# Two smaller buffers for the sums of the expert stage, and one sum written over its input

## The chip, the cores and the metric

The kernel runs on one core of a Trainium2 chip. The metric is the time of one execution on the device, in microseconds (us), as a median over runs; less is better. Profiles are of one further execution each.

## What is computed

Three parts follow each other. The output of the first is split up by tokens for the second, and the output of the second is the input of the third (N = 12288 tokens, width 256):

```python
# attention, per batch of 3072 tokens
attn = np.maximum(matmul(z, z.T) / S, 0.0) ** 2
x = u * matmul(attn, v)
# experts: each token goes to the one expert of 8 with the largest logit
h = np.maximum(x[mask] @ w1[e], 0.0)
out[mask] = gate_w[mask, None] * eom[mask, e, None] * (h @ w2[e])
# gated MLP with a product over the sequence
h = np.maximum(x @ w_in, 0.0)
u, v = h[..., :512], h[..., 512:]
v_n = (v - mean(v)) / sqrt(var(v) + 1e-6)
v_s = einsum('ts,bsd->btd', w_spatial, v_n) + b_spatial[None, :, None]
return (u * v_s) @ w_out
```

## The kernel before

The kernel holds every product as three matmuls of high and low parts. The product with w_spatial is made by a scheme with seven products in place of eight, on two levels, and that scheme needs sums and differences of blocks of w_spatial. They depend on no other input, so they are made early, as side work: `first_sums` beside the attention, and `spatial_sums` (from L714 on) beside the experts. Their results go to tensors in HBM, `w_sums` and `w_parts`, which the last part reads.

The experts run in `moe` (L602). 8 experts have 4 chunks of up to 512 tokens each, and each chunk has 8 steps f, so there are 256 steps i. A step makes on PE the first layer of (c, f) into a PSUM bank (L667 to L669), on ACT `hh` (L671), on DVE `hlo` (L673), and then on PE the second layer of two steps earlier (L620 to L622, called l2 below), which reads that earlier step's hh and hlo. When f is 7 the second layer's accumulators are emptied, by ACT (L630) and by DVE (L632) in turn, and an indirect transfer of POOL's queue scatters each to `y_tok` (L494). At the end of a step side work is pumped: one piece each of four generators, and `spatial_sums` is the last of them. A piece ends at a `yield`.

`spatial_sums` runs over 2 halves tb and 6 blocks k. For each k two rounds (th) load four tiles of 128 x 768 on SP's queue (L727, in the order a21, a22, a11, a12; a11 and a21 are of the tiles `sa` with four buffers, a22 and a12 of `sb` with three), make four whole sums on DVE (L731, L734, L736, L738), two of which POOL's queue stores to `w_sums` (L732, L739). The a11 of both rounds are then S2, the a21 of both rounds S3. Two groups follow, i = 1 on S2 and i = 2 on S3. A group splits its two tiles into halves of 384 columns (a11, a12 of the first, a21, a22 of the second), stores three of them as they are and makes four more blocks on DVE, L751, L754, L757 and L760, one in each of four pieces; every put (L747) is a transfer of POOL's queue to `w_parts`. Three of the four sums go to a tile `so` that has one buffer; the fourth, L754, writes over a21.

The order on PE, ACT, DVE and SP is that in which the program is written. POOL's order is made by a scheduler. Each engine's queue is worked off in order, and an instruction that waits holds up all that stand behind it. A tile's buffer is given to its next user when its last readers are done, transfers included.

Of the kernel before, what the change touches and what calls it, by code (L numbers as in the profile page):

```python
# [27 lines left out]
F32 = mybir.dt.float32  # L28
# [4 lines left out]
ALU = mybir.AluOpType  # L33
AX = mybir.AxisListType

P = 128
# [18 lines left out]
class _Kernel:  # L55
# [658 lines left out]
    def spatial_sums(self):  # L714


        nc, wk, tt = self.nc, self.big, self.nc.vector.tensor_tensor
        flat = self.sw.rearrange("n (s k) p t -> n k p s t", s=2)
        for tb in range(2):
            for k in range(6):  # L720
                S2, S3 = [], []
                for th in range(2):
                    tbs = 2 * th + tb
                    a11, a21 = (wk.tile([P, 768], F32, name="sa", bufs=4) for _ in range(2))
                    a22, a12 = (wk.tile([P, 768], F32, name="sb", bufs=3) for _ in range(2))
                    for dst, r, c in ((a21, 1, 0), (a22, 1, 1), (a11, 0, 0), (a12, 0, 1)):
                        nc.sync.dma_start(dst.rearrange("p (s t) -> p s t", s=2), self.wsq[r, c, tbs, k])  # L727
                    yield
                    yield
                    cs = slice(tbs * 384, tbs * 384 + 384)  # L730
                    tt(a22, a21, a22, op=ALU.add)  # L731
                    nc.gpsimd.dma_start(flat[0, k][:, :, cs], a22.rearrange("p (s t) -> p s t", s=2))  # L732
                    yield
                    tt(a21, a11, a21, op=ALU.subtract)  # L734
                    yield
                    tt(a11, a22, a11, op=ALU.subtract)  # L736
                    yield
                    tt(a12, a12, a11, op=ALU.subtract)  # L738
                    nc.gpsimd.dma_start(flat[1, k][:, :, cs], a12.rearrange("p (s t) -> p s t", s=2))  # L739
                    yield  # L740
                    S2.append(a11)
                    S3.append(a21)
                for i, (q, r) in ((1, S2), (2, S3)):
                    o = wk.tile([P, 1152], F32, name="so", bufs=1)
                    s1, s2, s4 = (o[:, n * 384 : n * 384 + 384] for n in range(3))
                    (a11, a12), (a21, a22) = ((t[:, 0:384], t[:, 384:768]) for t in (q, r))
                    put = lambda m, t: nc.gpsimd.dma_start(self.parts(i, m, tb, k), t)  # L747
                    put(1, a11)
                    put(2, a12)
                    put(4, a22)  # L750
                    tt(s1, a21, a22, op=ALU.add)  # L751
                    put(5, s1)
                    yield
                    tt(a21, a11, a21, op=ALU.subtract)  # L754
                    put(7, a21)
                    yield
                    tt(s2, s1, a11, op=ALU.subtract)  # L757
                    put(6, s2)
                    yield
                    tt(s4, a12, s2, op=ALU.subtract)  # L760
                    put(3, s4)
                    yield

    def produce(self):
# [598 lines left out]
```

## Time and profile before

| | us |
|---|---|
| median of 2 timed runs | 3648.74 (3648.63 to 3648.86) |
| the profiled execution | 3639.52 |
| its span, from first to last instruction | 3637.4 |
| attention, in that span | 0 to about 1186 |
| experts | about 1186 to 1842 |
| gated MLP | about 1842 to 3637 |

Times in the views are microseconds from the start of the span, if not marked ns. PE is the matmul engine, PEld its loading of weights, DVE the vector engine, ACT the scalar engine, POOL GpSimd, SP the sync engine; SP and POOL issue the transfers here (SPq and POOL in the rows). L751 is line 751 of the kernel. "out<-in" gives the tiles by the program's names.

### The profile page before, as it was taken

How to read it: one execution, taken by the hardware profiler on the slowest of the kernel's cores; microseconds unless marked ns; L12 is line 12 of the kernel's file. 1: busy time of each engine (PE TensorE's matmuls, PEld its weight loads, DVE VectorE, ACT ScalarE, POOL GpSimd, SP SyncE). 2: the span in 40 equal slices, each digit the busy share in tenths (PEclk: the TensorE clock that was granted, in tenths of full speed). 3: DMA queues.
4: the chain of work that ended last, by engine and by line, in shares of the span. 5: the costliest groups of instructions: out<-in, count | busy, mean ns of one | idle time of the engine just before them, and what ended most of it. 6: DMA issues, size and time to landing. Idle time of an engine off the chain costs nothing.

```text
span 3637.4 us, 48879 instructions
## 1 busy us (share of the span) xinstructions
PE 3522.8 (97%) x17680; PEld 3018.9 (83%) x17680; DVE 2507.1 (69%) x4541; ACT 1689.9 (46%) x2948; POOL 633.9 (17%) x861
## 2 busy tenths in 40 slices
PE   7999999999998899999999989999999999999999
PEld 6787787887886888989978879999988888888887
DVE  7989888888887567755557867576665556545544
ACT  6766777777775233333234443333333333323322
POOL 3213212113111334444322210000000000000000
PEclk9999999999999899999999999999999999999999
DMA  8212211102000666666447776768674567655543
GB/s 287 70 64 72 74 52 48 40 30 70 30 24 19 219 219 229 218 223 211 159 159 283 279 270 233 246 204 283 208 266 164 187 221 247 233 170 174 200 151 116
DMA packets 227454, 604.75 MB, mean 166 GB/s; under 512 B 24560, under 2 KB 62720, under 8 KB 227200
## 3 DMA queue, kind: packets, MB, share of 16 engines
q1 hardware_dynamic: 160032, 373.71, 30.7%
q0 software_dynamic: 67168, 227.81, 16.8%
q8 instruction: 140, 2.29, 0.3%
q14 instruction: 114, 0.93, 0.1%
HBM read 393.08 MB, written 208.35 MB: 165 GB/s over the span
## 4 chain that ended last, share of the span: by engine, by line
PE 77%; issue 8%; DVE 5%; DMA 5%; POOL 3%; ACT 2%; SPq 0%; DVEq 0%; POOLq 0%; ACTq 0%
PE bank L1212 7%; PE bank L1213 7%; PE bank L1211 7%; PE bank L228 6%; PE bank L229 6%; PE bank L227 5%; PE bank L1116 4%; PE bank L1115 4%; PE bank L1117 4%; PE bank L263 3%; PE bank L264 3%; PE bank L667 2%; PE bank L620 2%; PE bank L668 2%; PE bank L669 2%
## 5 line engine op out<-in xcount | busy, mean ns | idle before, releaser
L228 PE MATMUL bank<-lo,G 128*128 128x512 f32 x1152 | 455.9, 396 | 21.6 <-DVE lo L272 21.4
L1158 DVE TENSOR_TENSOR wl<-raw,wh 128x512 fp32r<-128x512 f32 x288 | 198.8, 690 | 397.4 <-ACT wh L1157 394.9
L272 DVE TENSOR_TENSOR lo<-a,hi 128x512 fp32r<-128x512 f32 x576 | 416.1, 722 | 76.1 <-PE bank L264 1.5
L266 ACT ACTIVATE r<-bank 128x512 f32<-128x512 f32 x576 | 343.1, 596 | 268.2 <-PE bank L264 244.1
L270 DVE TENSOR_TENSOR a<-r 128x512 f32<-128x512 f32 x576 | 414.0, 719 | 57.6 <-ACT r L266 56.5
L229 PE MATMUL bank<-hi,G 128*128 128x512 f32 x1152 | 452.6, 393 | 0.0
L227 PE MATMUL bank<-hi,G 128*128 128x512 f32 x1152 | 451.7, 392 | 0.0
L1157 ACT ACTIVATE wh<-raw 128x512 fp32r<-128x512 f32 x288 | 181.6, 631 | 534.3 <-PE bank L1213 484.4
L268 ACT ACTIVATE hi<-r 128x512 fp32r<-128x512 f32 x576 | 364.7, 633 | 18.3
L671 ACT ACTIVATE hh<-bank 128x512 fp32r<-128x512 f32 (+2 forms) x256 | 132.7, 519 | 431.6 <-PE bank L669 424.0
L1212 PE MATMUL bank<-wl,R 128*128 128x512 f32 x792 | 311.8, 394 | 2.1 <-DVE wl L1158 2.1
L1213 PE MATMUL bank<-wh,R 128*128 128x512 f32 x792 | 311.9, 394 | 0.0
L1211 PE MATMUL bank<-wh,R 128*128 128x512 f32 x792 | 311.9, 394 | 0.0
L228 PEld LDWEIGHTS bank<-lo,G 128*128 128x128 f32 x1152 | 217.5, 189 | 82.1 <-DVE lo L272 35.6
L673 DVE SCALAR_TENSOR_TENSOR hlo<-bank,hh 128x512 fp32r<-128x512 f32 (+2 forms) x256 | 150.9, 589 | 195.3 <-ACT hh L671 194.5
L227 PEld LDWEIGHTS bank<-hi,G 128*128 128x128 f32 x1152 | 217.2, 189 | 48.6 <-ACT hi L268 0.2
L229 PEld LDWEIGHTS bank<-hi,G 128*128 128x128 f32 x1152 | 217.4, 189 | 45.6
L1115 PE MATMUL bank<-wh,R 128*128 128x384 f32 x640 | 216.2, 338 | 13.5 <-ACT R L933 13.5
L620 PE MATMUL bank<-G,hh 128*128 128x256 f32 x728 | 208.0, 286 | 15.7 <-DVE in L632 15.0
L1116 PE MATMUL bank<-wl,R 128*128 128x384 f32 x640 | 216.1, 338 | 1.7 <-DVE wl L1184 1.7
L1117 PE MATMUL bank<-wh,R 128*128 128x384 f32 x640 | 215.9, 337 | 0.0
L399 POOL DMA_INDIRECT x_slots<-rows,slot x96 | 112.2, 1169 | 589.7 <-ACT r L266 519.0
(285 smaller groups left out, 8558.3 us busy)
## 6 DMA issues: line engine op xcount, KB each, us to landing
v_ops<-vu POOLq DMA_DIRECT2D x84, 512.0 KB, 4.5
raw<-w_parts SPq DMA_DIRECT2D x108, 384.0 KB, 3.5
ra<-v_ops SPq DMA_DIRECT2D x75, 512.0 KB, 4.4
raw<-wsp SPq DMA_DIRECT2D x72, 512.0 KB, 3.7
raw<-w_sums SPq DMA_DIRECT2D x72, 512.0 KB, 4.0
xin<-partial SPq DMA_DIRECT2D x60, 512.0 KB, 5.5
u_hid<-vu POOLq DMA_DIRECT2D x48, 512.0 KB, 3.9
ur<-u_hid SPq DMA_DIRECT2D x48, 512.0 KB, 6.9
```

The costliest lines, as they stand in the source:

```text
L227: nc.tensor.matmul(acc[d], vh[:, c], hi, start=(k == 0), stop=False)
L228: nc.tensor.matmul(acc[d], vh[:, c], lo, start=False, stop=False)
L229: nc.tensor.matmul(acc[d], vl[:, c], hi, start=False, stop=(k == NK - 1))
L268: nc.scalar.activation(hi, r, AF.Square)
L270: nc.vector.tensor_tensor(a, r, r, op=ALU.mult)
L272: nc.vector.tensor_tensor(lo, a, _f(hi), op=ALU.subtract)
L1115: nc.tensor.matmul(ps, vh, wh[:, ws], start=(k == 0), stop=False)
L1116: nc.tensor.matmul(ps, vh, wl[:, ws], start=False, stop=False)
L1117: nc.tensor.matmul(ps, vl, wh[:, ws], start=False, stop=(k == 5))
L1211: nc.tensor.matmul(acc[d], vh, wh, start=(k == 0), stop=False)
L1212: nc.tensor.matmul(acc[d], vh, wl, start=False, stop=False)
L1213: nc.tensor.matmul(acc[d], vl, wh, start=False, stop=(k == 11))
```

## The change

`so` becomes a tile of two blocks in place of three, with two buffers in place of one. The third sum of a group, L760, is written over its input a12, and put(3) sends a12. The sizes of the other tiles, the loops and the pieces stay.

```diff
                 for i, (q, r) in ((1, S2), (2, S3)):
-                    o = wk.tile([P, 1152], F32, name="so", bufs=1)
-                    s1, s2, s4 = (o[:, n * 384 : n * 384 + 384] for n in range(3))
+                    o = wk.tile([P, 768], F32, name="so", bufs=2)
+                    s1, s2 = (o[:, n * 384 : n * 384 + 384] for n in range(2))
                     (a11, a12), (a21, a22) = ((t[:, 0:384], t[:, 384:768]) for t in (q, r))
                     put = lambda m, t: nc.gpsimd.dma_start(self.parts(i, m, tb, k), t)
                     put(1, a11)
...
                     put(6, s2)
                     yield
-                    tt(s4, a12, s2, op=ALU.subtract)
-                    put(3, s4)
+                    tt(a12, a12, s2, op=ALU.subtract)
+                    put(3, a12)
                     yield
```

No row of an engine moves on PE, ACT, DVE and SP; what rows wait for does. DVE, where the first k's group i = 1 ends and group i = 2 begins (DMASW is a transfer of POOL's queue, DMAHW one of SP's, the other names are engines):

```order
 L673 SCALAR_TENSOR_TENSOR hlo<-bank_67,hh 128x512 [waits Activation_49]
 L185 TENSOR_TENSOR G_115<-raw_12936,G_114 128x512 [waits Activation_49]
-L760 TENSOR_TENSOR so<-sa,so 128x384 [waits DVE_49]
+L760 TENSOR_TENSOR sa<-sa,so 128x384 [waits DMASW5_49,DVE_49]
 L673 SCALAR_TENSOR_TENSOR hlo<-bank_66,hh 128x384 [waits Activation_49]
-L751 TENSOR_TENSOR so<-sa 128x384 [waits DMASW3_49,DMASW5_49,DMASW1_49,DVE_49]
+L751 TENSOR_TENSOR so<-sa 128x384
 L673 SCALAR_TENSOR_TENSOR hlo<-bank_67,hh 128x384 [waits Activation_49]
 L632 TENSOR_SCALAR in_13075<-bank_68,gate 128x256 [waits PE_49]
```

The three transfers are off the row of L751, and one is on the row of L760.

SP, a little later, the four loads of the second k's second round and what stands around them:

```order
 L504 DMA rows<-x_slots 128x1032 [waits PE_49]
-L727 DMA sa<-wsq 128x768 [waits DMASW5_49,DMASW3_49,DVE_49]
+L727 DMA sa<-wsq 128x768 [waits DMASW3_49,DVE_49]
 L727 DMA sb<-wsq 128x768 [waits DMAHW7_49,DMASW0_49]
-L727 DMA sa<-wsq 128x768 [waits DMAHW0_49,DVE_49]
+L727 DMA sa<-wsq 128x768 [waits DMAHW0_49,DMASW5_49,DVE_49]
 L727 DMA sb<-wsq 128x768 [waits DMAHW1_49,DMAHW2_49,DMASW6_49,DVE_49]
 L504 DMA rows<-x_slots 128x1032 [waits PE_49]
```

The third load, that of a11, has a transfer of POOL's queue added to what it waits for. The names DMASW are eight counters that are used in turn.

POOL, around the end of the first k's group i = 1 (a scatter is L494, a load of expert weights L419):

```order
 L747 DMA w_parts<-so 128x384 [waits DMASW3_49,DVE_49]
 L419 DMA raw_13547<-w 128x1024 [waits DMASW4_49,DVE_49]
-L747 DMA w_parts<-so 128x384 [waits DMASW5_49,DVE_49]
-L494 DMA y_tok<-in_13075,ids 26624x256 [waits DMASW6_49,Activation_49]
-L747 DMA w_parts<-so 128x384 [waits DMASW7_49,DVE_49]
-L494 DMA y_tok<-in_13075,ids 26624x256 [waits DMASW0_49,Activation_49]
+L747 DMA w_parts<-sa 128x384 [waits DMASW5_49,DVE_49]
+L747 DMA w_parts<-so 128x384 [waits DMASW6_49,DVE_49]
+L494 DMA y_tok<-in_13075,ids 26624x256 [waits DMASW7_49,Activation_49]
+L494 DMA y_tok<-in_13075,ids 26624x256 [waits DMASW0_49,DVE_49]
```

The put of the new first sum (`so`) stands ahead of the scatters instead of among them; the put ahead of it is the one that sends a12, of `sa`.

## Rows read from the trace of the kernel before

**Rows 1.** The page: the span, and each engine's busy time.

```profile
span 3637.4 us, 48879 instructions
PE 3522.8 (97%) x17680; PEld 3018.9 (83%) x17680; DVE 2507.1 (69%) x4541; ACT 1689.9 (46%) x2948; POOL 633.9 (17%) x861
```

**Rows 2.** Windows: length, busy PE, PEld, DVE, ACT, POOL, PE's clock, DMA share, GB/s.

```profile
1200.00:1843.00 643.00, 613.01 (x4163) 577.74 (x4162) 398.08 (x753) 208.63 (x421) 257.84 (x348) 0.98 0.58 201
1560.00:1595.00 35.00, 35.00 (x258) 34.22 (x257) 23.09 (x43) 11.61 (x26) 14.74 (x21) 1.00 0.62 223
```

**Rows 3.** Waits from 1200 to 1843: who, for whom, total, times, longest.

```profile
DVE so L751 <- DMA w_parts<-so: 46.6, 10, 8.8
...
PE bank L620 <- DVE in L632: 21.5, 5, 6.6
...
PE bank L667 <- DVE hlo L673: 7.7, 3, 3.6
DVE so L751 <- issue: 6.7, 1, 6.7
```

**Rows 4.** Timeline of DVE: start, length, work, idle time ahead of it.

```profile
1234.74 0.55 DVE L760 TENSOR_TENSOR so<-sa,so 128x384 f32<-128x384 f32 x1
...
1245.30 0.56 DVE L751 TENSOR_TENSOR so<-sa 128x384 f32<-128x384 f32 x1 [8.83 <-DMA w_parts<-so]
...
1246.24 0.87 DVE L632 TENSOR_SCALAR in<-bank,gate 128x256 f32<-128x256 f32 x2
...
1252.14 0.55 DVE L760 TENSOR_TENSOR so<-sa,so 128x384 f32<-128x384 f32 x1
```

**Rows 5.** Timeline of POOL, whose instructions here issue transfers.

```profile
1200.63 1.11 POOL L747 DMA_DIRECT2D w_parts<-sa  x2
1203.42 1.07 POOL L747 DMA_DIRECT2D w_parts<-sa  x2 [1.68 <-DVE sa L736]
...
1237.91 0.54 POOL L747 DMA_DIRECT2D w_parts<-so  x1
...
1252.98 0.55 POOL L747 DMA_DIRECT2D w_parts<-so  x1 [1.18 <-DVE so L760]
```

**Rows 6.** Timeline of PE around the same stall.

```profile
1238.85 0.28 PE L621 MATMUL bank<-K,hh 128*128 128x256 f32 x1
1238.97 0.28 PE L622 MATMUL bank<-K,hlo 128*128 128x256 f32 x1
...
1246.86 0.55 PE L620 MATMUL bank<-K,hh 128*128 128x256 f32 x1 [6.57 <-DVE in L632]
1247.21 0.42 PE L621 MATMUL bank<-K,hh 128*128 128x256 f32 x1
1247.43 0.41 PE L622 MATMUL bank<-K,hlo 128*128 128x256 f32 x1
```

**Rows 7.** Windows of the seven stretches at a lower clock: the first, and the sum.

```profile
1242.80:1253.00 10.20, 6.14 (x26) 6.17 (x27) 4.25 (x9) 0.49 (x1) 4.75 (x7) 0.50 0.34 133
...
sum 30.60, PE 26.17 PEld 25.34 DVE 19.73 ACT 3.49 POOL 16.85; mean PE 3.74 PEld 3.62 DVE 2.82 ACT 0.50 POOL 2.41
```

**Rows 8.** Landing of `so` puts; L754's durations in ns (min/median/max).

```profile
DMA to landing us min/median/max: 2.1/3.7/8.7
...
L754 DVE TENSOR_TENSOR sa<-sa x24: 546/549/573, 1229.0 to 1807.9; 128x384 f32<-128x384 f32 x24
```

**Rows 9.** SP's loads at L727: their landing, and the timeline of one.

```profile
DMA to landing us min/median/max: 2.9/4.7/10.5
...
1235.33 0.33 SPq L727 DMA_DIRECT2D sa<-wsq  x1
```

**Rows 10.** Timeline of DVE: from an L760 to the next L734.

```profile
1502.06 0.55 DVE L760 TENSOR_TENSOR so<-sa,so 128x384 f32<-128x384 f32 x1
...
1506.13 0.56 DVE L751 TENSOR_TENSOR so<-sa 128x384 f32<-128x384 f32 x1 [1.82 <-DMA w_parts<-so]
...
1518.07 0.94 DVE L734 TENSOR_TENSOR sa<-sa 128x768 f32<-128x768 f32 x1
```

## The prediction

> **What bounds the kernel now.** I read the page's busy line first: PE is busy for 97% of the span, DVE for 69%, POOL for 17% [rows 1]. A change in DVE or POOL work moves the end only where PE stands still for it. So the next view is the stretch in which the changed lines run, the experts, from 1200 to 1843 us: 643.00 us long, PE busy in 613.01 of them [rows 2]. PE loses 30.0 us there. A stretch between the losses is busy in every microsecond (35.00 of 35.00), with POOL and DVE at work as elsewhere [rows 2]. So what makes PE stop is something that happens at some places only.
>
> The table of waits says what [rows 3]. PE's own waits in this stretch are 21.5 us at L620 for DVE's L632 (5 times) and 7.7 us at L667 for the hlo of L673 (3 times): 29.2 of the 30.0 us are waits for DVE. DVE's row in the same table is L751 `so<-sa`, the first sum of a group: 46.6 us in 10 waits for the landing of a `w_parts<-so` transfer, and 6.7 us in one more whose ender is not named: 53.3 us in 11 waits.
>
> One of them in order of time [rows 4]: L760 of the first group runs at 1234.74; L751 of the second group, one hlo later in DVE's queue, runs at 1245.30, after 8.83 us of idle time. The reason is the one buffer of `so`: the second group's s1 goes where the first group's s4 has just been written, so it may start only when put(3) has read s4 out. POOL issued that put at 1237.91 [rows 5], so it took some 7 us to land. Behind L751 on DVE stand an hlo and the two L632 that empty the accumulators of l2. PE goes on at 1246.86 after 6.57 us of idle time, 0.6 us after the first L632 [rows 6].
>
> The stall has a second price. The granted clock is 0.50 of full from 1242.80 to 1253.00, that is 1.2 GHz and not 2.4, after PE had stood still; six later stalls leave 3.4 us each. The seven stretches are 30.60 us and hold 26.17 us of PE work [rows 7]. Behind the stall it takes 0.22 us from the start of an L621 to that of the L622 after it, against 0.12 us ahead of it [rows 6].
>
> **The change, step by step.**
>
> *The wait of L751 goes.* With two buffers of `so` a group writes where the group before last has written, a whole k earlier. The order of DVE shows it: the row of L751 waited for three transfers and waits for none. All 24 groups lose the wait; 11 of them had stalled. What comes back on PE is the idle time, 30.0 us, and the slow clock. At half clock a stretch of PE work takes twice as long, so 26.17 us of it at 0.50 are 13.1 us lost. Sum: 30.0 + 13.1 = 43.1 us.
>
> Here a rule of the Trainium skill can be set beside the rows. The page "TensorE: Matmul & The Clock Gate", section Terms, puts the penalty of a throttled clock at the throttled time times the share of pulses left out. The stretches together are 30.60 us, which by that would be 15.3 us, and the sum 45.3. I go by the PE work inside them, since 4.4 of these microseconds are idle time that stands in the 30.0 already.
>
> *The rows of DVE, ACT and PE stay in their places.* No instruction is added. L760 now writes over one of its inputs; L754 does that already, and takes 549 ns in the middle [rows 8] against the 0.55 us of an L760 [rows 4]. Cost: nothing.
>
> *L760 waits for put(2).* It overwrites a12, which put(2) sends out, so it now waits for that transfer. Price if it were just behind: up to 8.7 us, the longest landing of a `so` put [rows 8], at 24 places. Where the put stands: POOL's order is made by the scheduler and not by hand, and it issues puts 1 and 2 as soon as the whole sums of L734 and L736 are there. In the trace these are two pairs of `w_parts<-sa` [rows 5]: the one at 1203.42, released by L736, is of the first group, 31 us ahead of its L760 at 1234.74; the one at 1200.63 is of the second, 51 us ahead of its L760 at 1252.14 [rows 4]. Cost: nothing; the cover is over three times the longest landing.
>
> *SP's third load waits for put(3).* The tile that holds a12 is loaded anew for the next k. Before, that load needed only DVE's L760 to be over (SP issued it at 1235.33 [rows 9], the moment L760 ended); now it needs the landing of put(3). The order of SP shows the added transfer on the third of four loads. Behind it in SP's queue stand one more load, the `rows` of a later chunk, and the next group's loads. The delay: POOL issues put(3) some 0.3 to 2.6 us after L760 (1234.74 + 0.55 to 1237.91 is 2.6, 1252.69 to 1252.98 is 0.3 [rows 4, 5]), and it lands 2.1 to 8.7 us later, 3.7 in the middle [rows 8]. So 2.4 to 11.3 us, then the load itself: 4.7 us in the middle, 10.5 at the longest [rows 9]. Who waits for it: DVE at L734. The shortest distance that I found between an L760 and the L734 that needs the load is 1502.61 to 1518.07, 15.5 us, and a stall of 1.82 us inside it goes, which leaves 13.6 [rows 10]. In the middle 0.3 + 3.7 + 4.7 = 8.7 us are needed, so 4.9 are left over; at the worst of everything, 21.8, the load is 8.2 us late there. The other distances are longer. I take 0 to 1 us in all, nearest to the middle values, and keep the bound from the other side for the range.
>
> *POOL.* The put of s4 becomes a put of a12, of the same 128 x 384 numbers. In its queue put(5) of the second group now stands ahead of a chunk's scatters and so ahead of them waits for L751; but L751 itself comes some 9 us earlier than the 1245.30 of [rows 4]. POOL is busy 17% of the span; nothing is added there.
>
> The sum, against the profiled execution: 3639.5 (span 3637.4 [rows 1] and 2.1 around it) - 43.1 + 0.5 = 3596.9. The timed runs have a median of 3648.7, 9.2 us above the profiled one; no row tells why, and I carry the difference over unchanged: 3648.7 - 43.1 + 0.5 = 3606.1, said as **3606 us**, 1.2% below the time before.
>
> **The rivals.**
>
> *A, the forecast (0.74).* All 11 stalls go with their slow clock: 3600 to 3614. For it: 29.2 of PE's 30.0 us of idle time are waits for DVE, and DVE has no other wait for a transfer there [rows 2, 3].
>
> *B, part of it comes back as another wait (0.13).* The load behind put(3) is late in some groups, so that DVE stalls at L734 in place of L751; or the half-clock stretches stay where a small stop is left. Eleven stalls cost PE 43.1 us, 3.9 each; with a third to two thirds of them replaced the time is 3620 to 3635. For it: put(3) and SP's loads share the DMA engines, and the distance of 13.6 us can be used up. Against it: the middle values leave 4.9 us even at the tightest place.
>
> *C, nothing is gained (0.07): 3644 to 3652.* The wait of L751 would be replaced by one of equal length at the next DVE instruction, because something else on POOL or SP arrives just after put(3). Against it: behind L751 come L673 and L632, which need only ACT and PE, and in the first stall L632 began 0.94 us behind L751 with no idle time ahead of it [rows 4].
>
> *D, slower (0.04).* One mechanism: SP's queue. If landing and load together take more than the distance in every group, DVE stalls at all 22 later L734 where it now stalls at 11 L751. At 3.9 us each that is 86 us, and 3606 + 86 = 3692. It decides from 13.6 us on at the tightest place, against 8.7 needed in the middle. The change ends on the wrong side once 12 such stalls are there.
>
> The rest (0.02) is a larger gain than A's, for instance if the timed runs hold more of these stalls than the profiled one: their 9.2 us more would bring 3597.
>
> **How the numbers follow.** The time is A's. The range goes down to the 3597 of the last case and up into B, to 3632, where A and most of B lie inside and C, D and the end of B (some 0.15) outside. Faster by over 2% (about what a measurement of this kernel can tell from no change) would be below 3575.8, a gain of 73 us; PE's whole idle time in the stretch is 30.0, so 0.01. Slower by over 2% is above 3721.7, more than D gives: 0.01. Within 2%: 0.98.
>
> **What would show it.** In the profile of the changed kernel L751 has no DVE wait for `w_parts`; PE is busy in all but 1 or 2 us of the experts; no half-clock stretch lies between 1200 and 1800; the experts end near 1800 and not 1843; SP issues the third load of a group 3 to 8 us after L760. It would be wrong if L734 or L760 show DVE waits for a DMA, or if PE stops at L620 for another reason that these stalls now hide.

## The result and the profile after

| us | before | after |
|---|---|---|
| median of the timed runs | 3648.74 (3648.63 to 3648.86) | 3600.05 (3599.4 to 3600.7) |
| the profiled execution | 3639.52 | 3599.4 |
| its span | 3637.4 | 3597.6 |

The changed kernel takes 0.987 of the time before, with a 95% interval of 0.985 to 0.989. The forecast was 3606, the range 3597 to 3632. The profiled execution of before is one beside its timed runs; that of after, and of every kernel below, is one of its timed runs.

The page of after, the lines that answer to [rows 1]:

```profile
span 3597.6 us, 48893 instructions
PE 3512.8 (98%) x17680; PEld 3011.3 (84%) x17680; DVE 2509.9 (70%) x4541; ACT 1690.6 (47%) x2948; POOL 632.2 (18%) x861
```

DVE, ACT and POOL are as busy as before. PE is busy for 10 us less, though it runs the same 17680 matmuls.

The experts of both kernels as windows, each from the first matmul of the first layer to the last of the second (length, busy PE, PEld, DVE, ACT, POOL, PE's clock, DMA share, GB/s). First before, then after:

```profile
1188.40:1845.00 656.60, 626.60 (x4233) 588.99 (x4232) 405.56 (x764) 212.92 (x428) 258.81 (x349) 0.97 0.59 204
```

```profile
1189.90:1802.30 612.40, 612.29 (x4233) 577.31 (x4232) 406.49 (x764) 212.97 (x429) 257.46 (x349) 1.00 0.63 218
```

The same 4233 matmuls take 44.2 us less. Idle time of PE was 656.60 - 626.60 = 30.0 us and is 0.1; busy time fell by 626.60 - 612.29 = 14.3 us. PE comes out of the attention at half clock (0.50) in both kernels, which covers the first 3.2 us of the experts of before and the first 2.4 of after; behind that the clock is 1.00 to the end of the experts of after. The span fell by 39.8 and not by 44.2, because the attention took 1.5 us more and the gated MLP 3.0 us more in this execution.

The waits of after from 1200 to 1800 (who, for whom, total, times, longest), to be held against [rows 3]:

```profile
ACT hh L671 <- PE bank L669: 375.6, 248, 2.7
DVE hlo L673 <- ACT hh L671: 198.0, 213, 2.6
...
POOL w_parts L747 <- DVE so L751: 16.8, 15, 2.8
```

PE has no row in this table, and DVE has none for a transfer. The two largest rows are the chain that PE feeds: ACT waits for PE's banks, and DVE for ACT.

The place of the first stall, DVE and then POOL (start, length, work), to be held against [rows 4, 5]:

```profile
1235.91 0.55 DVE L760 TENSOR_TENSOR sa<-sa,so 128x384 f32<-128x384 f32 x1
...
1237.55 0.55 DVE L751 TENSOR_TENSOR so<-sa 128x384 f32<-128x384 f32 x1
...
1240.02 0.87 DVE L632 TENSOR_SCALAR in<-bank,gate 128x256 f32<-128x256 f32 x2
```

```profile
1239.08 0.54 POOL L747 DMA_DIRECT2D w_parts<-sa  x1
1239.61 0.54 POOL L747 DMA_DIRECT2D w_parts<-so  x1
```

L751 runs 1.64 us after L760 where it ran 10.56 us after it, and ahead of put(3), which POOL issues at 1239.08. L632 follows without a stop.

### The profile page after: what moved, and what is told of

Same layout as the page of the kernel before. It is cut to its first block, busy times and chain, and to the rows that moved or that the text cites. A ratio compares the mean times of both kernels' runs of the same rounds, so it can differ in the third digit from the quotient of the medians.

```text
span 3597.6 us, 48893 instructions
## 1 busy us (share of the span) xinstructions
PE 3512.8 (98%) x17680; PEld 3011.3 (84%) x17680; DVE 2509.9 (70%) x4541; ACT 1690.6 (47%) x2948; POOL 632.2 (18%) x861
## 4 chain that ended last, share of the span: by engine, by line
PE 83%; issue 5%; DVE 5%; DMA 4%; POOL 2%; ACT 2%; SPq 0%; DVEq 0%; POOLq 0%; ACTq 0%
PE bank L1213 7%; PE bank L1212 7%; PE bank L1211 7%; PE bank L228 6%; PE bank L229 6%; PE bank L227 6%; PE bank L1116 4%; PE bank L1117 4%; PE bank L1115 4%; PE bank L263 3%; PE bank L264 3%; PE bank L622 3%; PE bank L621 3%; PE bank L620 3%; PE bank L667 3%
## 5 line engine op out<-in xcount | busy, mean ns | idle before, releaser
L622 PE MATMUL bank<-G,hlo 128*128 128x256 f32 x728 | 205.7, 283 | 0.0
```

## The experiments

No kernel leaves out any of the work. T in the expectations is the mechanism of the prediction: put(3) holds the one `so`, DVE waits at L751, PE stops behind DVE and then runs at half clock. Medians are compared where the kernel before ran beside them on the same chip: 3640.87 us beside the first four kernels, 3647.13 beside the next four, 3645.57 beside the last four.

The stages of every profiled execution, counted from the trace as above: attention, experts and gated MLP ("rest"); in the experts PE's idle time, the PE work done at half clock (without the 1.6 to 3.2 us that each kernel brings over from the attention), and the idle time plus half of that work:

```
                         attention  experts  rest    idle  at half  idle + half
before                     1188.4    656.6  1792.4   30.0   26.3     43.2
after                      1189.9    612.4  1795.4    0      0        0
e1_again                   1189.3    611.9  1791.8    0      0        0
e2_three_tiles             1187.8    612.2  1798.8    0      0        0
e3_in_place_one_buffer     1188.8    615.2  1800.0    1.9    0        1.9
e4_one_more_piece          1192.9    626.3  1802.0    9.6    6.7     13.0
e5_one_piece_less          1193.9    672.6  1796.3   43.4   28.9     57.9
e6_short_way               1190.8    622.5  1795.5    6.8    6.5     10.0
e7_short_way_a11_first     1189.0    635.1  1794.5   15.4   12.8     21.8
e8_short_three_a11_first   1190.8    625.8  1799.3   10.2    3.4     11.9
e9_before_again            1188.0    651.8  1800.4   28.6   19.8     38.5
e10_again                  1188.4    612.4  1799.2    0      0        0
e11_over_a21               1194.1    638.7  1802.5   16.5   18.6     25.8
e12_over_s2                1191.9    640.5  1801.9   20.7    6.4     23.9
```

Experts without a stop take 611.9 to 612.4 us. Every other length is 612.2 plus the last column and some 0.3 to 4.4 us more; what these last microseconds are stays open. Attention and gated MLP differ by 6 and 11 us over the table, though no edit touches them. Between repeats of one kernel the attention differs by at most 1.5 us, the gated MLP by 8.0. The profiled execution is not always near the median of its kernel: e1_again's lies 7.4 us below, e7's 7.3 below, e11's 9.6 above, e4's 5.7 above.

### The result once more, and the kernel before

e1_again and e10_again are the changed kernel, e9_before_again the kernel before.

> The changed kernel once more, timed in rounds for an interval. Theory T (PE loses time in the experts only where DVE waits at L751 for put(3), as idle time and then as slow clock): 3596 to 3606, 40 to 50 below the kernel before of the same chip, no DVE wait for w_parts, PE busy from 1200 to 1800 without a gap, no half clock there. Rival R1 (a part of the gain was chance of one execution): under 30 below, or gaps of PE in this profile.

> The changed kernel once more, beside the two below on one chip. T: 0.988 to 0.991 of the kernel before; experts of 611 to 613 us in the profile, no gap of PE there.

> The kernel before once more, for a second profile of it beside the others. T: 9 to 12 DVE waits at L751, 45 to 65 us in all, PE gaps of 25 to 35 us in the experts and 20 to 35 us of slow clock there, experts of 652 to 660 us; what one execution has more than another lies in the attention and in the gated MLP. Rival: the stalls differ much from one execution to the next (experts of under 645 or over 665), and with them the times of 3637 to 3649.

Rows of waits are from here on those of the stretch from 1195 to 1835 us (who, for whom, total, times, longest). Measured: 3602.14 against 3640.87 (0.990, interval 0.9875 to 0.9925), 38.7 us less; 3604.46 against 3645.57 (0.9888, interval 0.9872 to 0.9905), 41.1 us less. With the first pair's 48.7 these are three sizes of one gain; 38.7 is just under the 40 to 50 that T foretold for e1_again. e9_before_again took 3642.35, and its experts are just under the 652 to 660 foretold. The experts of the changed kernel took 612.4, 611.9 and 612.4 us, those of the kernel before 656.6 and 651.8; what the profiles show beyond that lies in the two other stages. The waits of the repeated kernel before, in the experts:

```profile
DVE so L751 <- DMA w_parts<-so: 45.1, 10, 8.0
...
PE bank L620 <- DVE in L632: 19.9, 6, 5.8
...
DVE so L751 <- issue: 7.1, 1, 7.1
```

These are the rows of [rows 3] again: 52.2 us in 11 waits against 53.3 in 11. The stalls belong to the kernel and not to one execution. What varies is the work at half clock behind them, 19.8 us here and 26.3 there (26.17 by [rows 7]), and with that and 1.4 us of idle time the length of the experts, by 4.8 us.

### Which part of the edit is it?

e2_three_tiles keeps the kernel before, with one buffer and s4 as a block of its own, and only makes three tiles of one:

```diff
-                    o = wk.tile([P, 1152], F32, name="so", bufs=1)
-                    s1, s2, s4 = (o[:, n * 384 : n * 384 + 384] for n in range(3))
+                    s1, s2, s4 = (wk.tile([P, 384], F32, name=f"so{n}", bufs=1) for n in range(3))
```

> The kernel before, but s1, s2 and s4 are three tiles of 384 columns with one buffer each: no more memory than before, and L760 does not write over a12. T: L751 now waits only for put(5) of the group before, which is four pieces old (6 to 11 us), so the stalls go, and the time is that of the changed kernel within 3 us. Rival R2 (the third load, which in the changed kernel waits for put(3), costs something there): 2 to 6 below the changed kernel, since here that load waits for DVE alone. Rival R3 (a second buffer is needed): within 10 us of the kernel before.

Measured: 3601.93, ratio 0.9898 (0.9872 to 0.9923), equal to e1_again to 0.2 us. DVE's waits for a transfer in its experts, all of them (its lines stand one higher, L759 is L760 and L756 is L757):

```profile
DVE so L759 <- DMA w_parts<-so: 2.9, 2, 2.3
DVE so L756 <- DMA w_parts<-so: 1.0, 1, 1.0
```

And the place of the first stall on its DVE:

```profile
1233.71 0.55 DVE L759 TENSOR_TENSOR so<-sa,so 128x384 f32<-128x384 f32 x1
...
1235.35 0.55 DVE L750 TENSOR_TENSOR so<-sa 128x384 f32<-128x384 f32 x1
...
1244.89 0.56 DVE L759 TENSOR_TENSOR so<-sa,so 128x384 f32<-128x384 f32 x1 [2.33 <-DMA w_parts<-so]
```

The first sum again runs 1.64 us behind the last one. So no second buffer is needed for the gain. In the kernel before the three sums were blocks of one tile, and a tile is given on as a whole: s1 had to wait for the put of s4, though s1's own block had been sent out long before. With a tile for each sum, s1 waits only for put(5) of the group before, which is four pieces old. That the changed kernel is no slower than this one, which has no wait of SP's load for put(3), also shows that this new wait costs nothing.

e3_in_place_one_buffer is the changed kernel with one buffer of `so`:

```diff
-                    o = wk.tile([P, 768], F32, name="so", bufs=2)
+                    o = wk.tile([P, 768], F32, name="so", bufs=1)
```

> Only the second part of the change: L760 writes over a12, and so has two blocks but one buffer. L751 of the second group then waits for put(6) in place of put(3). In the trace of before put(6) landed 4.2 and 4.9 us after DVE was ready for L751 in two groups, 0.8 to 1.7 us in four, before it in four. T: DVE waits of 12 to 20 us in all, PE gaps of 3 to 8 us, with a slow stretch or two 3606 to 3614, that is 6 to 12 above the changed kernel. Rival R4 (any wait for a put at that place costs as much): 3635 to 3649.

Measured: 3605.7, ratio 0.9909 (0.9883 to 0.9935), 3.6 us above e1_again. Now s1 waits for put(6), which is one piece older than put(3). Its DVE waits in the experts:

```profile
DVE so L751 <- issue: 6.6, 2, 4.4
...
DVE so L751 <- DMA w_parts<-so: 2.8, 2, 1.9
```

With two single ones of 0.5 and 0.4 us these are 10.3 us in 6 waits, and PE stops for only 1.9 us. All three sizes lie below what T foretold (waits of 12 to 20 us, gaps of 3 to 8, 6 to 12 above the changed kernel), so the way was right and the price set too high. By the experts' length (615.2 us against 612.2) writing s4 over a12 alone brings all but 3 us of the 44, and the second buffer brings those 3; the timed runs of the two kernels overlap and can't show so small a difference.

### How the price follows the age of put(3)

The generator runs one piece for each step of the experts, so a `yield` more or less moves L751 away from put(3) or towards it. Both kernels are the one before, with one edit:

```diff
# e4_one_more_piece
                     yield
+                    if i == 1:
+                        yield
# e5_one_piece_less
-                    yield
+                    if i == 2:
+                        yield
```

> The kernel before with one buffer of so, but one more bare yield between the two groups, so that L751 of the second group comes one step (1.4 to 2.8 us) later in DVE's order. T: every stall of DVE is shorter by that step; of 53 us some 25 to 32 remain, in 7 or 8 places; PE, which bears 1.5 to 3 us of a stall without a gap, loses 8 to 18 us and some slow clock: 3608 to 3628. Rival R5 (the put lands a fixed time after L751 is reached, since DVE or POOL are released by each other): the stalls stay, 3640 to 3650.

> The kernel before with the yield between the two groups taken away, so that L751 of the second group stands right behind L760 of the first in DVE's order. T (a stall is the landing of put(3) less what DVE does between L760 and L751): each stall is longer by one step, 1.4 to 2.8 us, and all 12 stall: DVE waits of 75 to 90 us at L751 in place of 53, PE gaps of 45 to 55 in place of 30, and slow clock behind nearly all of them: 3655 to 3680, 15 to 40 above the kernel before of the same chip. Rival R6 (PE gets the time back because the sums end earlier): within 5 us of the kernel before.

e4 measured 3617.3, ratio 0.993 (0.9906 to 0.9954): a piece of distance more, and 23.6 of the 38.7 us that the changed kernel gains on this chip are there. Its DVE rows, of the experts, and the one of PE:

```profile
DVE so L751 <- DMA w_parts<-so: 15.6, 5, 6.7
...
PE bank L667 <- DVE hlo L673: 9.6, 5, 4.5
...
DVE so L751 <- issue: 8.2, 2, 5.0
```

e5 measured 3664.61, ratio 1.0057 (1.0036 to 1.0077): slower, by 17.5 us. Its DVE and PE rows:

```profile
DVE so L751 <- DMA w_parts<-so: 73.3, 12, 9.0
PE bank L667 <- DVE hlo L673: 34.0, 9, 6.9
...
PE bank L620 <- DVE in L632: 9.3, 3, 6.9
```

All 12 places between two groups of a k now stall. Ordered by distance, DVE waits 73.3 (e5), 53.3 (before), 24.4 (e4; eight waits with a single one of 0.6), and PE's idle time is 43.4, 30.0, 9.6. The chain from put(3) to PE holds in both directions. e5's idle time and its DVE waits are just below what was expected for them (45 to 55 and 75 to 90).

### Is the new wait on SP hidden by luck?

In the changed kernel the third load waits for put(3). Two pieces lie between the loads and L731; without them the loads have less time. e6_short_way is the changed kernel without the two bare `yield` lines behind the loads, and e7_short_way_a11_first also asks for a11 first:

```diff
# e7; e6 has only the two lines that go
-                    for dst, r, c in ((a21, 1, 0), (a22, 1, 1), (a11, 0, 0), (a12, 0, 1)):
+                    for dst, r, c in ((a11, 0, 0), (a21, 1, 0), (a22, 1, 1), (a12, 0, 1)):
                         nc.sync.dma_start(dst.rearrange("p (s t) -> p s t", s=2), self.wsq[r, c, tbs, k])
-                    yield
-                    yield
```

e8_short_three_a11_first is e7's edit on e2's kernel, in which no load waits for put(3). It is the control.

> The changed kernel without the two bare yields between a round's loads and its first sum: the distance from L760 to the L734 that needs the third load shrinks by two steps, 2.9 to 5.6 us. In the changed kernel's trace the loads landed 3.7 to 21 us before their sums, so that 0 to 3 places come out 0 to 2 us short. T: DVE waits at L731 and L734 of 0 to 5 us in all, PE without a gap: the changed kernel's time within 4 us. Rival D (the wait of the load for put(3) is close to costing): gaps of PE, 3608 to 3630.

> As e6, and SP loads a11 first, so that all four loads of a round stand behind the wait for put(3). put(3) lands 2.6 to 9 us after L760 and two loads another 4 to 6, against 9 to 20 us to L731 without the bare yields. T: here the wait costs: 4 to 10 of the 22 later L731 wait for a load, 10 to 30 us in all, of which PE shows a third to a half, with some slow clock: 5 to 20 above the changed kernel. Rival N (the wait for put(3) never costs, since DVE's order has room enough): within 3 us of it.

> The control of e7: the same loads and pieces, but three tiles of 384 columns as in e2, so that no load waits for put(3), only for L760. T: the difference between e7 and this one is the price of the wait for put(3) where it is tight: this one 4 to 15 below e7, within 5 of the changed kernel. Rival: if the short way alone does it, e8 is as slow as e7.

e6 measured 3610.16, ratio 0.9902 (0.9875 to 0.9929). It gains 37.0 us on the kernel before of its chip, where the changed kernel gained 38.7 and 41.1 on two others, so the medians alone do not show it slower. In its profile the experts are 10.3 us longer than without a stop, and DVE's waits (9.4 us in 4) are above the 0 to 5 foretold. The expectation of T that PE has no gap missed. The rows of DVE and PE in its experts, and one of the places on DVE (its lines stand two higher, L729 is L731):

```profile
DVE sb L729 <- DMA sb<-wsq: 9.4, 4, 3.6
...
PE bank L620 <- DVE in L632: 5.8, 2, 3.1
```

```profile
1351.69 0.96 DVE L729 TENSOR_TENSOR sb<-sa,sb 128x768 f32<-128x768 f32 x1 [3.56 <-DMA sb<-wsq]
```

The second load of that round, a22, on SP:

```profile
1343.24 0.42 SPq L727 DMA_DIRECT2D sb<-wsq  x1
```

It took 8.4 us until L729 could start. It is not the load that waits for put(3). The load ahead of it went out at 1342.82, when put(7) had landed (1342.75) and 5.5 us before put(3) did (1348.35), so SP's queue was not held for put(3) there. So this stall is the price of the missing pieces: with them the loads of every round had landed before their sums.

e7 measured 3627.7, ratio 0.9953 (0.9939 to 0.9967); e8 measured 3616.03, ratio 0.9917 (0.9892 to 0.9942). Their rows for L729, e7 first:

```profile
DVE sb L729 <- DMA sb<-wsq: 23.3, 10, 5.2
```

```profile
DVE sb L729 <- DMA sb<-wsq: 9.6, 5, 2.5
...
DVE sb L729 <- DMA w_parts<-so: 2.9, 1, 2.9
```

The last row names a put, but that L729 starts 0.12 us after a load of a22 has landed, as the others do: the control has 12.5 us in 6 waits there. And SP's queue at one place of each, the same round of loads (a row of x2 holds two loads), e7 first, with the row of POOL that issues put(3) and the L729 that needs the loads:

```profile
1344.10 6.13 SPq L727 DMA_DIRECT2D sa<-wsq  x2
1350.28 0.91 SPq L727 DMA_DIRECT2D sb<-wsq  x2
```

```profile
1343.57 0.54 POOL L745 DMA_DIRECT2D w_parts<-sa  x1
```

```profile
1354.61 0.96 DVE L729 TENSOR_TENSOR sb<-sa,sb 128x768 f32<-128x768 f32 x1 [5.20 <-DMA sb<-wsq]
```

And the control:

```profile
1343.62 0.84 SPq L727 DMA_DIRECT2D sa<-wsq  x2
1344.51 1.32 SPq L727 DMA_DIRECT2D sb<-wsq  x2
```

```profile
1353.47 0.96 DVE L729 TENSOR_TENSOR sb<-sa,sb 128x768 f32<-128x768 f32 x1 [2.91 <-DMA w_parts<-so]
```

In e7 the second `sa` load holds SP's queue for 6 us (put(3), for which it has to wait, was issued at 1343.57 and landed at 1349.84), and the load of a22 behind it starts at 1350.28; in the control nothing holds it, and it starts at 1344.51. Not all of these 5.8 us are lost: L729 starts only 1.1 us later, since the earlier load takes longer to land (8.8 us against 4.2). The difference of the two kernels, 11.7 us by medians and 9.3 in the experts, is the price of the wait for put(3) where nothing covers it; DVE waits 23.3 us in 10 places against 12.5 in 6. It is an approximate price, since the control also waits 3.9 us for puts at two of its three small sums, which e7 does not. So the wait is real, and the changed kernel does not pay for it because its order of loads and its two pieces cover it. The control itself is 13.6 us longer in the experts than e2, and 7.6 to 10.0 us short of the changed kernel's gains on other chips, where at most 5 was foreseen: the two pieces cover more than this wait.

### Could the sum be written over something else?

The third sum has other operands that are no longer needed. e11_over_a21 writes it over a21, whose put(7) is two pieces old, and e12_over_s2 over s2, whose put(6) is one piece old:

```diff
# e11_over_a21
-                    tt(a12, a12, s2, op=ALU.subtract)
-                    put(3, a12)
+                    tt(a21, a12, s2, op=ALU.subtract)
+                    put(3, a21)
# e12_over_s2
+                    tt(s2, a12, s2, op=ALU.subtract)
+                    put(3, s2)
```

> The changed kernel, but L760 writes over a21 in place of a12, and put(3) sends a21. L760 then waits for put(7), which is two pieces old (2.9 to 5.6 us), where put(2) was 25 us and more. T (the wait of L760 costs nothing only since put(2) is so old): DVE waits at L760 of 8 to 25 us in all, PE gaps of 1 to 8 us, 2 to 12 above the changed kernel. Rival (writing over an input is free whatever it waits for): within 1 us.

> The same with s2: L760 writes over s2, which put(6) sends one piece earlier (1.4 to 2.8 us). A put lands 2.1 to 8.7 us after its issue. T: L760 waits in most of the 24 groups, 40 to 80 us in all; PE bears 1.5 to 3 us of each, so gaps of 10 to 30 us and some slow clock: 12 to 45 above the changed kernel, at the upper end slower than the kernel before. Rival (as in e11): within 1 us.

e12 measured 3633.23, ratio 0.9964 (0.9949 to 0.9979), 28.8 us above e10_again and inside what was expected. e11 measured 3627.56, ratio 0.994 (0.9919 to 0.9962), 23 us above e10_again, twice what was expected at most. Its four runs lie 20 us apart, and the profile is of the slowest, 3637.19. The waits of DVE in the experts, e12 and then e11:

```profile
DVE so L760 <- DMA w_parts<-so: 73.3, 22, 8.1
...
PE bank L667 <- DVE hlo L673: 19.9, 11, 3.9
```

```profile
DVE sa L760 <- DMA w_parts<-sa: 48.8, 15, 7.0
...
PE bank L667 <- DVE hlo L673: 16.2, 6, 4.6
```

Why a put that should be two pieces old is late shows on e11's POOL queue, with the DVE row that waits for it behind:

```profile
1244.66 1.01 POOL L494 DMA_INDIRECT y_tok<-in,ids  x1 [0.45 <-ACT in L630]
1245.97 0.99 POOL L494 DMA_INDIRECT y_tok<-in,ids  x1 [0.30 <-issue]
1247.27 0.96 POOL L494 DMA_INDIRECT y_tok<-in,ids  x1 [0.30 <-DVE so L757]
1248.53 0.96 POOL L494 DMA_INDIRECT y_tok<-in,ids  x1 [0.30 <-DMA w_parts<-sa]
1249.50 0.58 POOL L747 DMA_DIRECT2D w_parts<-sa  x1
```

```profile
1255.72 0.56 DVE L760 TENSOR_TENSOR sa<-sa,so 128x384 f32<-128x384 f32 x1 [6.90 <-DMA w_parts<-sa]
```

The put of L754's sum stands behind four scatters of a chunk and is issued at 1249.50, although L754 had run at 1244.87. L760, which was next on DVE from 1248.8 on, could start only at 1255.72, when the put had landed, 6.1 us after its issue. In the 24 groups of e11, 9 have three or four scatters ahead of this put; it is issued 3.1 to 5.2 us after L754 there (0.3 us where there is none), and these 9 hold 41 of the 48.8 us. What counts for a write over a tile is when its put leaves POOL's queue and has landed, and not how many pieces ago the sum was made. Of the three places, a12 is the one whose put was issued before the group began.

## Why the prediction came out

**The wait of L751 goes, with all it brings.** Right. L751 has no wait in after; e2 to e5 show put(3) and the shared tile as its cause. The step's 43.1 us were 44.2: idle time 30.0 as read, and 14.3 us of PE's busy time where the step had 13.1 us of slow clock. Some 0.4 of the 1.2 us between them is chance: the half clock brought over from the attention was 3.2 us long in before and 2.4 in after. The rest stays open.

**The rule beside it.** The Trainium skill's page "TensorE: Matmul & The Clock Gate", section Terms, gave an estimate of 15.3 us for the slow clock and 45.3 for the sum. The 14.3 us of PE's busy time that went lie between that and the 13.1. The sum of 44.2 is 1.1 from either, so this case does not choose between the full length of the stretches and the work inside them.

**The rows stay, and L760 in place costs nothing.** Right. All 24 of after, in ns (min/median/max), beside the 549 of [rows 8]:

```profile
L760 DVE TENSOR_TENSOR sa<-sa,so x24: 540/551/554, 1235.9 to 1770.3; 128x384 f32<-128x384 f32 x24
```

**L760's wait for put(2) costs nothing.** Right for the reason given: no L760 of after has idle time ahead of it for a transfer. e11 and e12 show what the same kind of wait costs where the put is young: 48.8 and 73.3 us of DVE's time. A version in which put(2) itself is late was not tried.

**SP's third load waits, and it is covered.** Right. SP in after, the place of [rows 9]:

```profile
1233.16 0.33 SPq L727 DMA_DIRECT2D sa<-wsq  x1
1233.53 1.10 SPq L727 DMA_DIRECT2D sb<-wsq  x1
1243.63 0.33 SPq L727 DMA_DIRECT2D sa<-wsq  x1
```

The third load starts 7.2 us after the end of L760 (1235.91 + 0.55), where before it started at once. Over the groups this is 2.6 to 9.0 us, against 3 to 8 foretold, and at the tightest place 4.3 us are left before L734, against the 4.9 worked out. That the two are so near is luck: they belong to different places. At the prediction's own place the stall inside the distance went, but 15.5 us were left and not 13.6, and 7.2 over. The other distances are not all longer: the shortest of after is 13.0 us, from 1712.62 to 1725.65, with 5.3 over, and the tightest place has a distance of 19.3 us, of which the third load's late issue (7.8 us) and its landing (7.2 us) take most. The step's price was set at 0.5 us and was nothing. Where the cover is gone it is 9.3 to 11.7 us (e7 against e8).

**The time itself.** 3600.05 is 6 us below the forecast. The step that was off is the last: the 9.2 us by which the timed runs before lay above the profiled one were carried over unchanged. After's two timed runs, one of them profiled, lie 1.3 us apart. The single executions of the kernel before went from 3635 to 3653 us on these chips, those of the changed kernel from 3595 to 3610. Part of that is seen in the table of stages: between repeats the gated MLP differs by 8.0 us (before) and 7.4 (after), and the experts of before by 4.8. No execution of before above 3642.35 was profiled, so where the rest of the spread lies stays open, and that the 9.2 us were one draw of it is the likely reading and not shown. Beside the kernel before of the same chip the gain was 38.7 and 41.1, against 42.6 foretold; the 48.7 of the first pair is the largest of the three, so that its closeness to the range's lower end is in part chance.

**The rivals.** A held, though 3600.05 is the very edge of its 3600 to 3614 and nearer to the 3597 of the case of a larger gain than to 3606. Whether the slower runs of before hold more of these stalls, as that case supposes, no profile shows; e9_before_again has the same ones. B's mechanism, a late load, cost nothing here, but e6 shows how near it lies: two pieces less, and the loads make PE idle for 6.8 us. C would have shown another DVE wait; there is none. D's condition never came up, and its price of 3.9 us for each stall was high for such a wait: in e7 ten late loads, some of them late without put(3) too, made the experts 22.9 us longer, 2.3 each.

## What to carry to other kernels

Where blocks of one tile are sent out one after the other, the first write of the next round waits for the last put of all; a tile for each block takes that wait away without any more memory, and may be tried before a second buffer. Before a result is written over an operand, look up when that operand's last transfer leaves its queue, since three or four scatters ahead of it in the queue outweighed two steps of age here. An engine that is busy for 97% of the span may still lose 44 us in one stage: add up its idle time there, see which engine it waits for, then what that one waits for, and add what the clock takes after each stop.

## What the runs showed of the hardware

The slow clock (0.50, that is 1.2 GHz) does not follow the length of the stop before it. In the kernel before PE stood still for 3.59 us ahead of 1602.96 without a loss of clock, and for 1.82 us ahead of 1405.92 with one. The windows around both places (columns as above):

```profile
1400.00:1412.00 12.00, 10.18 (x58) 9.26 (x58) 6.49 (x12) 3.48 (x7) 2.13 (x4) 0.86 0.82 320
1595.00:1610.00 15.00, 11.41 (x79) 10.34 (x78) 6.50 (x15) 4.19 (x9) 4.90 (x9) 1.00 0.84 265
```

The clock was 0.86 in the mean of the first, which holds 3.4 us at 0.50, and 1.00 (2.4 GHz) in the second. In their experts e12 stops 20.7 us in 14 gaps and has 6.8 us at half clock, e11 stops 16.5 us in 7 gaps and has 20.5. So the two kernels lose nearly the same (640.5 and 638.7 us in the experts) by different shares.

A stall of DVE also costs PE less than its length: e3's 10.3 us of DVE waits, in six pieces of up to 4.4 us, gave 1.9 us of idle PE, before 53.3 gave 30.0, and e2's 3.9 in three gave none. The likely reason is that PE still has work that does not need the stalled sums. An estimate of what was free in each stall, from these numbers: (53.3 - 30.0) / 11 is 2.1 us before, (73.3 - 43.4) / 12 is 2.5 in e5, and (10.3 - 1.9) / 6 is 1.4 in e3, where some stalls were shorter than that.
